# Loading each row of v once and copying the neighbour rows inside the v tile

## The chip, the cores and the metric

One core of one Trainium2 chip runs the whole program. The metric is the device time of one execution in microseconds. The kernel before took 333.7 us (median of 3 runs, 332.48 to 333.8).

## The reference, cut to what matters

Two stages follow each other. The first is attention in chunks: 4 batches, 8 heads, 768 positions, 64 numbers per head. A chunk of 32 queries sees its own 32 keys, 16 to the left, 8 to the right, and 8 memory keys of its head.

```python
for c in range(nc):                      # 24 chunks of 32
    l_start = max(0, c * 32 - 16)
    r_end = min(S, c * 32 + 32 + 8)
    k_full = concat([mem_k, k[:, :, l_start:r_end]])
    v_full = concat([mem_v, v[:, :, l_start:r_end]])
    a = softmax(scale * q_c @ k_full.T)
    out[:, :, c * 32:c * 32 + 32] = a @ v_full
```

The second stage is a mixture of 8 experts over the 3,072 tokens that come out (512 numbers each). Logits with noise choose two experts for each token, a softmax over the two gives their weights, and each expert is `relu(x @ w1) @ w2` with a hidden size of 1,024.

```python
noisy = x @ w_gate + log1p(exp(x @ w_noise)) * noise
top2 = the two largest per token; top2_w = softmax over the two
out[token] = sum over the two of top2_w * (relu(x @ w1[e]) @ w2[e])
```

## The kernel before

*Attention.* The 32 heads are taken in 8 groups of four heads, and a group in two pairs of heads. For a group, POOL issues the loads of q and k (L505, `qk_load`, 384 KB each as counted in the tile) and two loads of v (L516, `piece` inside `v_load`), one for each half of the partitions. All three convert from float32 to bfloat16 on the way.

The tile of v is `vg`, [128 partitions, 2, 48 chunks, 66]. A half has 64 partitions, and each partition is one position in the window of a chunk: 16 left neighbours, the chunk's 32 own positions, 8 right neighbours (`WIN` is 56 in all) and 8 memory rows. The third axis is the chunk: 24 of one head and 24 of the next. The last axis holds the 64 numbers of v, a column of ones (which gives the sum of the softmax) and a spare column. So the product with v for one chunk takes all its rows from one column block, and a position that is a neighbour of another chunk lies in the tile twice. The load writes all 56 rows of every chunk, so v's rows are read 56/32 times over. Where a window runs over the edge of the tensor, an extra short load takes its place (`first`, `last`).

Three v tiles (`NV = 3`) take turns, and so do three each of q and k. Group g + 3 uses the tile of group g, once the second pair's product has read it. At the start the tiles are cleared, and the column of ones is set.

The memory rows come from a copy that is already in SBUF (`memv`, inside the tile `XS`): two transfers of 49.5 KB for a group, issued by SyncE (SP) on its own DMA queue (L535, `mem_rows`).

For each pair, PE turns q and k (L555), makes the scores (L578 for memory, L585 for the window), DVE takes the maximum off (L592, L608), ACT takes the exponential (L611), PE turns the result (L617) and multiplies with v (L631, 24 products, one for a chunk), DVE normalises into `xrow` (L635, L647) and PE turns that for the logits (L656). After four pairs a batch is done and its routing follows (L693 to L907): logits, choice of two experts, places in a table. SP writes the batch's rows to `x_rows` in DRAM (L913).

*Experts.* When a table is ready, POOL gathers rows of `x_rows` (L949), PE turns them (L980) and multiplies with w1 (L1055), ACT or DVE takes the positive part (L1065, L1067), PE multiplies with w2 (L1096), DVE adds with the gate (L1107, L1115), and POOL scatters to the output (L1127). The weights w1 of the first two experts have tiles of their own (`w1t`, loaded on L927) beside the attention tiles; the other weight tiles (`w1l`, `w2l`) use memory that the attention leaves.

*The order.* A planner written in Python (`Planner.run`) lays all operations out ahead of time. Each has the engines that may do it with a duration, what it depends on (`deps`), what it must only be issued after (`after`), buffers that it takes and uses, and a priority. The priority is a formula plus a correction from the table `SHIFT` by name, and by name and running number. The instruction order of each engine, the DMA queues included, is the planner's, and the real waits are set by the data. `FETCH` is a part of the planner's model: per 128 products PE spends at least the third number of microseconds up to the time in the fourth, and the fifth number after it. A DMA has a transfer time and a latency in the model (`dma=`). The first w1 load is put after the list that group 5 keeps of its v operations, the second after that of group 7 (`groups[NG - 3][5]`, `groups[NG - 1][5]`). Before, that list is the two loads and the memory rows. The product with v depends on the same list.

Of the kernel before, what the change touches and what calls it, by code (L numbers as in the profile page):

```python
# [22 lines left out]
FETCH = (128, 94, 6.3, 97.0, 3.2)  # L23
SHIFT = {
# [183 lines left out]
def kernel(  # L208
# [14 lines left out]
    nc = tc.nc  # L223
    B, H, S, D = q.shape
    n_mem = mem_k.shape[2]
    chunk, left_ctx, right_ctx = 32, 16, 8
    ncnk = S // chunk
# [158 lines left out]
    z_v = []  # L386
# [111 lines left out]
    for g in range(NG):  # L498
# [11 lines left out]
        def v_load(o, hh, bv=bv, g=g, h0=h0, b=b):  # L510
            vt = bv.t
            hd = b * H + h0 + 2 * hh
            p0 = 64 * hh

            def piece(c, n, j=0, nj=WIN):
                G_.dma_start(out=vt[p0 + j:p0 + j + nj, hh, c:c + n, :D],  # L516
                             in_=bass.AP(v.tensor, v.offset + (hd * S + c * chunk + j - left_ctx) * D, [[D, nj], [chunk * D, n], [1, D]]))

            first, last = hd == 0, hd == B * H - 2
            if first:  # L520
                piece(0, 1, left_ctx, WIN - left_ctx)
            if last:
                piece(2 * ncnk - 1, 1, 0, WIN - right_ctx)
            piece(int(first), 2 * ncnk - first - last)
# [742 lines left out]
```

## Time and profile before

| What | us |
|---|---|
| profiled execution, its own time | 333.6 |
| its span, first to last instruction | 332.1 |
| PE busy (matmuls) | 282.3 |
| DVE busy | 159.8 |
| ACT busy | 147.9 |
| POOL busy | 131.3 |
| first product with v (L631) starts | 27.9 |
| first product of the experts (L1055) starts | 121.8 |

The table is read thus: times inside the execution count from the start of the span, and the execution's own time is 1.5 us longer than the span. Mean granted clock of PE over the span: 0.903. Of the DMA queues, the one that POOL issues to moved 38.78 MB in 74,672 packets, SP's queue 4.19 MB in 5,014.

### The profile page before, as it was taken

To read this page: it belongs to the slowest core of one execution; us is meant where nothing else is said; L and a number is where in the kernel's file an instruction comes from. 1 tells how busy PE (TensorE), PEld (TensorE's weight loads), DVE (VectorE), ACT (ScalarE), POOL (GpSimd) and SP (SyncE) were. 2 spreads that over 40 slices of the span, in tenths; PEclk is the share of its full clock that TensorE was granted. 3 is DMA by queue.
4 is the path that set the end of the run, shared out by engine and by line. 5 is a ranking of instruction groups with operands and counts; after the bars stand their busy time and mean duration, and the time that the engine had idled before them with its cause. 6 is when DMAs were issued, how large, how long until landed. Compare 5 with 4: busy or idle time off the path is not lost.

```text
span 332.1 us, 7279 instructions
## 1 busy us (share of the span) xinstructions
PE 282.3 (85%) x2972; PEld 177.1 (53%) x2972; DVE 159.8 (48%) x372; ACT 147.9 (45%) x261; POOL 131.3 (40%) x178
## 2 busy tenths in 40 slices
PE   0587588777567679999999999999999999999991
PEld 0575366665446456664646655545545744744540
DVE  7776677888748776824313431144042041043041
ACT  8675667888264134760611417403703604603500
POOL 7767533345000776987282410132032032051072
PEclk9999975978755558999999999999999999999998
DMA  7999999999999359289999910699613621021032
GB/s 100 208 128 139 149 150 149 212 171 195 223 183 116 89 127 177 79 140 188 247 210 227 248 68 0 106 182 198 101 54 78 99 79 57 2 109 51 3 122 82
DMA packets 80013, 43.55 MB, mean 131 GB/s; under 512 B 53805, under 2 KB 73262, under 8 KB 79974
## 3 DMA queue, kind: packets, MB, share of 16 engines
q0 software_dynamic: 74672, 38.78, 100.2%
q1 hardware_dynamic: 5014, 4.19, 4.9%
q8 instruction: 24, 0.39, 0.5%
q14 instruction: 15, 0.12, 0.1%
q10 hardware_dynamic: 288, 0.07, 0.1%
HBM read 61.26 MB, written 10.85 MB: 217 GB/s over the span
## 4 chain that ended last, share of the span: by engine, by line
PE 59%; DMA 21%; issue 8%; POOL 4%; DVE 4%; ACT 1%; POOLq 1%; DVEq 0%; ACTq 0%
PE ps_l L1055 20%; DMA vg<-in_v_dram 19%; PE ps_l L1096 18%; PE ps_g L1096 7%; PE ps_g L1055 7%; PE ps_l L980 2%; POOL out_dram L1127 2%; PE ps_o L631 2%; DMA kn<-in_k_dram 2%; PE ps_g L656 1%; DVE xrow L647 1%; POOL vg L516 1%; POOLq L1183 1%; PE ps_g L617 1%; PE ps_s L585 1%
## 5 line engine op out<-in xcount | busy, mean ns | idle before, releaser
L1065 ACT ACTIVATE ht<-ps_l 128x384 bf16<-128x384 f32 (+2 forms) x110 | 48.5, 491 | 95.0 <-PE ps_l L1055 94.0
L1096 PE MATMUL ps_l<-w2l,ht 128*128 128x512 bf16 x328 | 73.7, 379 | 0.0
L1096 PEld LDWEIGHTS <-ht 128*128 128x128 bf16 x448 | 43.6, 98 | 51.5
L1127 POOL DMA_INDIRECT out_dram<-acc,oid x28 | 28.8, 1028 | 84.9 <-DVE acc L1115 79.7
L1115 DVE SCALAR_TENSOR_TENSOR acc<-ps_l,gates,acc 128x512 f32<-128x512 f32 x22 | 16.5, 751 | 60.3 <-PE ps_l L1096 59.3
L1055 PEld LDWEIGHTS <-w1t 128*128 128x128 bf16 x416 | 31.4, 100 | 19.6 <-issue 2.2
L1055 PE MATMUL ps_l<-XS,w1t 128*128 128x384 bf16 (+4 forms) x312 | 40.7, 285 | 0.7 <-ACT XS L368 0.7
L1055 PEld LDWEIGHTS <-w1l 128*128 128x128 bf16 x320 | 29.9, 98 | 19.1
L1055 PE MATMUL ps_l<-XS,w1l 128*128 128x512 bf16 (+3 forms) x240 | 39.9, 316 | 0.0
L516 POOL DMA_DIRECT2D vg<-in_v_dram x18 | 23.7, 1317 | 23.3 <-DMA vg<-in_v_dram 10.7
L368 ACT COPY kT<-ps_q 64x768 bf16<-64x768 bf16 x31 | 24.6, 793 | 8.8 <-PE ps_q L555 8.2
L1096 PE MATMUL ps_g<-w2l,ht 128*128 128x512 bf16 x120 | 28.2, 379 | 0.0
L555 PE MATMUL ps_q<-identb,qn 128*64 128x128 bf16 x192 | 11.9, 276 | 15.6 <-POOL identb masks.py:199 10.6
L631 PE MATMUL ps_o<-vg,PT 128*32 128x132 bf16 x384 | 12.1, 279 | 9.0 <-DMA vg<-in_v_dram 5.0
L1107 DVE TENSOR_SCALAR acc<-ps_l,gates 128x512 f32<-128x512 f32 x13 | 9.8, 751 | 19.6 <-PE ps_l L1096 19.6
L1065 ACT ACTIVATE ht<-ps_g 128x384 bf16<-128x384 f32 (+2 forms) x38 | 16.8, 471 | 5.3 <-PE ps_g L1055 5.1
L949 POOL DMA_INDIRECT xl<-x_rows,gid x16 | 16.7, 1044 | 5.8 <-PE ps_l L980 2.2
L555 PEld LDWEIGHTS <-qn 128*64 128x64 bf16 x192 | 9.6, 147 | 16.6 <-DMA qn<-in_q_dram 12.6
L592 DVE TENSOR_REDUCE mx<-ps_s 128x12 f32<-128x768 f32 x16 | 15.3, 953 | 3.8 <-PE ps_s L585 3.4
L368 ACT COPY PT<-ps_g 128x768 bf16<-128x768 bf16 x13 | 10.3, 796 | 12.3 <-PE ps_g L617 11.2
L961 DVE COPY gates<-xl 64x8 f32<-64x8 f32 (+1 forms) x40 | 11.0, 292 | 9.9 <-DMA xl<-x_rows,gid 8.0
L647 DVE TENSOR_TENSOR xrow<-ps_o,rec 128x768 bf16<-128x768 f32 x16 | 15.3, 958 | 0.6
(179 smaller groups left out, 387.7 us busy)
## 6 DMA issues: line engine op xcount, KB each, us to landing
w2l<-in_moe_w_dram POOLq DMA_DIRECT2D x8, 1024.0 KB, 11.2
vg<-in_v_dram POOLq DMA_DIRECT2D x14, 336.0 KB, 20.9
w1t<-in_moe_w_dram POOLq DMA_DIRECT2D x4, 1024.0 KB, 22.3
w1l<-in_moe_w_dram POOLq DMA_DIRECT2D x4, 1024.0 KB, 10.5
kn<-in_k_dram POOLq DMA_DIRECT2D x8, 384.0 KB, 15.0
qn<-in_q_dram POOLq DMA_DIRECT2D x8, 384.0 KB, 18.7
x_rows<-xrow SPq DMA_DIRECT2D x2, 792.0 KB
x_rows<-xrow SPq DMA_DIRECT2D x2, 768.0 KB
```

The costliest lines, as they stand in the source:

```text
L368: A.copy(dst, src)
L516: G_.dma_start(out=vt[p0 + j:p0 + j + nj, hh, c:c + n, :D], in_=bass.AP(v.tensor, v.offset + (hd * S + c * chunk + j - left_ctx) * D, [[D, ...
L555: P_.transpose(out=dst.t[64 * hh:64 * hh + 64, t * QP:(t + 1) * QP], in_=s[:, j + 2 * hh, t, :], identity=identb)
L592: mx = op("mx", ("DVE", 0.98), lambda o, bmx=bmx, bS=bS: V.tensor_reduce(out=bmx.t, in_=sv(bS), axis=AX, op=Alu.max), deps=[sc], alloc=[bm ...
L631: P_.matmul(out=pvw[32 * r:32 * r + 32, u // UB, u % UB], lhsT=PT[:, u, 32 * r:32 * r + 32], rhs=vt[:, :, ncnk * j + c], start=True, stop= ...
L647: V.tensor_tensor(out=x5, in0=ov(bO)[:, :, :, :, :D], in1=r5.to_broadcast([128, 2, UB, 2, D]), op=Alu.mult)
L949: G_.indirect_dma_start(out=bx.t[:n], out_offset=None, in_=src, in_offset=bass.IndirectOffsetOnAxis(ap=ids_[:n, c:c + 1], axis=0), bounds_ ...
L1055: P_.matmul(out=dst, lhsT=w1b[e].t[:, kp, f * 128:(f + 1) * 128], rhs=src, start=(kp == 0), stop=(kp == KP - 1), skip_group_check=True)
L1065: A.activation(out=dst, in_=s_, func=Act.Relu)
L1096: P_.matmul(out=gy.t, lhsT=ht.t[:, f, j, :], rhs=w2b[e].t[:, f, :], start=(f == 0), stop=(f == FB - 1))
L1115: V.scalar_tensor_tensor(out=ba.t, in0=gy.t, scalar=gate, in1=ba.t, op0=Alu.mult, op1=Alu.add)
L1127: G_.indirect_dma_start(out=out_part[nv], out_offset=bass.IndirectOffsetOnAxis(ap=oid[:, c:c + 1], axis=0), in_=ba.t, in_offset=None, boun ...
```

## The change

Each v load now brings only the 32 own rows of a chunk, to the partitions 16 to 47 of its half, for all 48 chunks in one transfer; the extra short loads at the edges are gone. When a half has landed, SP issues two copies inside the tile. The first takes the last 16 of the own rows of chunk c (partitions 32 to 47) to the left neighbours (partitions 0 to 15) of chunk c + 1. The second takes the first 8 own rows (partitions 16 to 23) of chunk c + 1 to the right neighbours (partitions 48 to 55) of chunk c. Both move 47 chunks whole, 66 numbers each with the column of ones. The product with v now waits for the memory rows and the copies.

The planner's durations for the v load are changed, the copies are added to its list, `FETCH` has 6.9 in place of 6.3, and the table `SHIFT` is another one, so the order of nearly all instructions is new. The list of a group that the w1 loads are put after is now the memory rows and the two pairs of copies.

```diff
-FETCH = (128, 94, 6.3, 97.0, 3.2)
+FETCH = (128, 94, 6.9, 97.0, 3.2)
 SHIFT = {
...
         def v_load(o, hh, bv=bv, g=g, h0=h0, b=b):
             vt = bv.t
             hd = b * H + h0 + 2 * hh
-            p0 = 64 * hh
-
-            def piece(c, n, j=0, nj=WIN):
-                G_.dma_start(out=vt[p0 + j:p0 + j + nj, hh, c:c + n, :D],
-                             in_=bass.AP(v.tensor, v.offset + (hd * S + c * chunk + j - left_ctx) * D, [[D, nj], [chunk * D, n], [1, D]]))
-
-            first, last = hd == 0, hd == B * H - 2
-            if first:
-                piece(0, 1, left_ctx, WIN - left_ctx)
-            if last:
-                piece(2 * ncnk - 1, 1, 0, WIN - right_ctx)
-            piece(int(first), 2 * ncnk - first - last)
+            p0 = 64 * hh + left_ctx
+            G_.dma_start(out=vt[p0:p0 + chunk, hh, :, :D], in_=bass.AP(v.tensor, v.offset + hd * S * D, [[D, chunk], [chunk * D, 2 * ncnk], [1, D]]))
 
         zd = z_v[g] if g < NV else []
-        lv = [op("lv", ("POOL", 1.4 if 0 < g < NG - 1 else 2.2), lambda o, hh=hh, f=v_load: f(o, hh), deps=zd, alloc=[bv] if hh == 0 else [], use=[] if hh == 0 else [bv],
-                 prio=pr + 2 + 0.5 * hh, dma=(2.75, 1.6), tag="attn") for hh in range(2)]
+        lv = [op("lv", ("POOL", 1.05), lambda o, hh=hh, f=v_load: f(o, hh), deps=zd, alloc=[bv] if hh == 0 else [], use=[] if hh == 0 else [bv],
+                 prio=pr + 2 + 0.5 * hh, dma=(1.6, 1.6), tag="attn") for hh in range(2)]
...
-        groups.append((bq, bk, bv, lq, lk, lv + [lm]))
+
+        def spread(o, hh, bv=bv):
+            vt = bv.t[64 * hh:64 * hh + 64, hh]
+            nc.sync.dma_start(out=vt[:left_ctx, 1:], in_=vt[chunk:chunk + left_ctx, :2 * ncnk - 1])
+            nc.sync.dma_start(out=vt[left_ctx + chunk:WIN, :2 * ncnk - 1], in_=vt[left_ctx:left_ctx + right_ctx, 1:])
+
+        ln = [op("ln", ("SP", 0.3), lambda o, hh=hh, f=spread: f(o, hh), deps=[lv[hh]], after=[lm] if hh else [], use=[bv], prio=pr + 3 + 0.2 * (hh + 1), dma=(0.5, 1.8), tag="attn") for hh in range(2)]
+        groups.append((bq, bk, bv, lq, lk, [lm] + ln))
```

29 rows, old and new, of the table SHIFT are left out of this document.

## The prediction

> **What bounds the kernel now.** I read the page's slices first, then the busy times by stage, then the chain of waits, then the DMA queues. The slices, 8.3 us each:
>
> ```profile
> PE   0587588777567679999999999999999999999991
> DVE  7776677888748776824313431144042041043041
> PEclk9999975978755558999999999999999999999998
> DMA  7999999999999359289999910699613621021032
> ```
>
> From slice 15 on (about 122 us) PE is full: the experts. Before, nothing is full but the DMA engines, from 8 to about 98 us. So the change, which touches only the attention stage, is worth what it moves the start of the experts. The same by stage: length, then PE, PEld, DVE, ACT and POOL (busy us, instructions), clock, DMA share, GB/s:
>
> ```profile
> 27.86:81.64 53.78, 40.27 (x972) 32.94 (x972) 43.01 (x99) 39.17 (x56) 24.89 (x49) 0.82 2.45 167
> 59.29:81.64 22.35, 16.08 (x431) 13.46 (x422) 20.18 (x55) 19.09 (x28) 8.89 (x9) 0.88 1.91 197
> 81.64:98.68 17.04, 9.79 (x185) 8.08 (x182) 11.30 (x28) 7.62 (x13) 1.26 (x2) 0.60 1.91 205
> 98.68:121.78 23.10, 15.62 (x279) 12.66 (x279) 18.46 (x55) 7.97 (x14) 11.05 (x15) 0.50 0.77 114
> 121.78:127.50 5.72, 5.72 (x50) 4.03 (x50) 3.76 (x22) 1.58 (x4) 2.02 (x3) 0.50 0.90 107
> 127.50:325.00 197.50, 197.50 (x1255) 107.92 (x1253) 62.71 (x129) 71.04 (x160) 71.53 (x81) 1.00 0.57 118
> ```
>
> I cut the stages at PE's products with v (L631, 24 for a pair, 48 for a group): counted for that line alone, in the same stretches:
>
> ```profile
> 27.86:81.64 53.78, 7.31 (x240) 5.03 (x240) 0.82 2.45 167
> 81.64:98.68 17.04, 1.38 (x48) 0.93 (x48) 0.60 1.91 205
> 98.68:121.78 23.10, 3.41 (x96) 2.31 (x96) 0.50 0.77 114
> ```
>
> So groups 0 to 4 took 53.78/5 = 10.76 us each, group 5 took 17.04, and groups 6 and 7 with the end of the routing 23.10. The chain says what group 6 waited for:
>
> ```profile
> 48.42 20.39 DMA vg<-in_v_dram
> 71.15 27.49 DMA vg<-in_v_dram
> 98.68 0.85 PE ps_o L631 x18
> ```
>
> A v load issued at 71.15 lands 27.49 us later, and PE's product starts 0.04 us behind it. The groups before were slowed too, but less plainly.
>
> **The change, part by part.** *Loads.* A half load fell from 56 rows x 48 chunks = 2,688 pieces of 128 B to 32 x 48 = 1,536. What a piece costs, from two full stretches of 10 us (20 to 30, and 30 to 40):
>
> ```profile
> DMA packets 8222, 1.35 MB, mean 135 GB/s; under 512 B 7694, under 2 KB 8206, under 8 KB 8221
> q0 software_dynamic: 8189, 1.24, 303.6%
> q1 hardware_dynamic: 32, 0.10, 6.5%
> DMA packets 5537, 1.46 MB, mean 146 GB/s; under 512 B 4538, under 2 KB 5517, under 8 KB 5533
> ```
>
> With a for a small packet (v) and b for a middle one (q, k; 8206 - 7694 = 512 and 5517 - 4538 = 979): 7694a + 512b = 10 and 4538a + 979b = 10 give a = 0.90 ns, b = 6.1 ns. A half load thus costs 2.4 us of all engines, and 1.4 after: 1.03 saved, 2.06 for a group, 16.5 in all.
>
> [...]
>
> *Copies, added.* Per half one copy of 16 partitions and one of 8, whole rows of 47 x 66 x 2 = 6,204 B: 24 rows, 0.149 MB. Nearest row: the memory rows on the same queue, 0.10 MB in the 6.5% above (0.065 x 160 = 10.4 engine-us). By it a half's copies are 15.6 engine-us, 0.98 us of 16 engines if they ran alone, and 0.98/3.1 = 0.31 beside the 3.1 packets that are in flight per engine there. I take 0.5, nearer to the lower end since the loads do run beside it: 1.0 a group (0.6 to 2.0). Net per group -1.06 us of DMA time (-1.45 to -0.1).
>
> *Order of the w1 load.* It goes behind what the group's list ends with, which were load issues and is now the copies, planned behind the landing of the loads. Now, from POOL's timeline and the issues (KB, us to landing):
>
> ```profile
> 58.33 1.39 POOL L516 DMA_DIRECT2D vg<-in_v_dram  x1 [2.02 <-DMA vg<-in_v_dram]
> 60.48 0.78 POOL L927 DMA_DIRECT2D w1t<-in_moe_w_dram  x1
> 69.58 2.96 POOL L516 DMA_DIRECT2D vg<-in_v_dram  x2 [2.60 <-DMA vg<-in_v_dram]
> w1l<-in_moe_w_dram POOLq DMA_DIRECT2D x4, 1024.0 KB, 10.5
> ```
>
> The 1,024 KB go out at 60.48, right behind the loads of group 5 and ahead of the loads of group 6, which are late. The same size later, with the queue freer, lands in 10.5 us, so it is worth up to about 8 us of queue. Behind group 6's loads it costs nothing: the first expert product is at 121.78. With the 12 loads before group 6's second one (12 x 0.53 = 6.4) that is more than the 6.3 us by which group 5's stage is too long (17.04 - 10.76). I take the whole stall away: **-6.3** (0 to -6.3).
>
> *The pace of the other groups.* DMA time would let it fall by 1.06. DVE is busy 43.01/5 = 8.60 us per group, and where DMA pressed least (59.29 to 81.64) it was busy 20.18 of 22.35, 90%; at 90% a group takes 9.56, or 1.2 less than now. PE has a limit of its own:
>
> ```profile
> 33.34:41.40 8.06, 4.13 (x129) 3.13 (x129) 5.33 (x8) 5.00 (x7) 4.20 (x4) 1.00 2.78 150
> 41.40:48.69 7.29, 5.73 (x129) 4.90 (x129) 5.60 (x10) 4.96 (x8) 1.69 (x2) 0.77 2.86 149
> 41.40 0.35 PE L631 MATMUL ps_o<-vg,PT 128*32 128x132 bf16 x11 [2.29 <-issue]
> 48.69 0.30 PE L555 MATMUL ps_q<-identb,kn 128*64 128x128 bf16 x3 [1.20 <-issue]
> q8 instruction: 24, 0.39, 0.5%
> ```
>
> PE stops in the middle of a run of products, waiting for nothing that the profile shows, every 128 or so products, and a DMA queue named instruction brings 0.39 MB in 24 packets, 16 KB each. So PE's instructions come in blocks, and a block took 7.29 to 8.06 us while the engines were full. The copies do not lighten that, and the planner's figure for a block goes up from 6.3 to 6.9. Between no gain and 1.2 I take 0.7, nearer to what DMA and DVE allow, for each of seven groups: **-4.9** (0 to -8.4).
>
> *The first group.* It has no earlier work to hide the copies: SP waits for the second load, issues two copies (0.62 us each, as the memory rows on L535 below) and they land. The shortest landing that the trace has, of gathered rows, is 2.8 us. So +4.0, less the two shorter loads, 2.06: **+2** (-1 to +4). For later groups the copies lie under the groups ahead as long as v lands earlier than its use.
>
> ```profile
> L535 SPq DMA_DIRECT2D vg<-XS x16: 624/624/770, 11.5 to 74.9; - x16
> DMA to landing us min/median/max: 2.8/5.1/18.1
> 79.37 1.44 POOL L516 DMA_DIRECT2D vg<-in_v_dram  x1 [1.21 <-DMA vg<-in_v_dram]
> 86.50 34.95 SPq L913 DMA_DIRECT2D x_rows<-xrow  x4
> 109.75 1.17 POOL L949 DMA_INDIRECT xl<-x_rows,gid_s  x1 [14.22 <-DVE rec L635]
> ```
>
> *SP's queue.* SP now stands waiting for each half load, and behind it stand the next memory rows and the writes of x rows (L913). Their reader is the gather at 109.75. The last v load goes out at 79.37 and with the 20.9 us of the median (row under D) is in by about 100 even as things are, so the third write has some ten us of cover; I cost it at nothing, and without cover at what it is late. The 32 issues (20 us of SP) lie in SP's waiting. POOL's issues get shorter, but POOL is idle half of the time (24.89 of 53.78 busy): nothing.
>
> *The experts.* From 127.50 PE is busy all 197.50 us at full clock; their work is the same: nothing. The first 50 products run at clock 0.50 for 5.72 us, of which 2.9 could go if PE came warm; I take nothing.
>
> **Sum.** 333.6 us is the profiled execution's own time: a span of 332.1 and 1.5 around it, 0.1 under the median of the runs shown. 333.6 - 6.3 - 4.9 + 2.0 = **324.4**, say 324, with its own range 319 to 330.
>
> **The rivals.** *B, all of it gives.* The pace falls to DVE's 9.56 (-8.4), the stall goes (-6.3), the experts start warm (-2.9) and the first group one us sooner: 333.6 - 18.6 = 315. For it: a new order of everything, made for these costs; DMA share falls to 1.91 where loads are fewer and products come faster there (431 in 22.35 us, 6.6 us for 128). Against: DVE must stay at 90% throughout. [...]
>
> *C, PE's instructions bound.* From 27.86 to 121.78 PE does 972 + 185 + 279 = 1,436 products. At 8.06 us for 129 they take 89.7 us against 93.92 now: -4.2, +2 for the first group: 331.4. For it: the two stalls. Against: the pace of 59.29 to 81.64.
>
> *E, the copies eat it.* At 0.98 us a copy pair a group saves 0.1 us of DMA time; if the w1 load's place matters little, the stall stays: 333.6 + 2 - 0.7 = 334.9.
>
> *D, slower: the copies sit in the turn of the v tiles.* There are three; a tile is free only after its second pair's product. Group 3's first load goes out at 33.17 and group 6's, into the same tile, at 69.58. Loads now also need the copies to land, L us later, and two turns follow each other. Each costs L - 2.1 more. With L at half of a v load's 20.9 us, 10.5, as one of several queues under a full engine: 2 x 8.4 = +16.8, less the 9.2 of the forecast: 341. It decides from L = 2.1 + 9.2/2 = 6.7 us. Against: the shortest landing, 2.8.
>
> ```profile
> 33.17 1.41 POOL L516 DMA_DIRECT2D vg<-in_v_dram  x1
> vg<-in_v_dram POOLq DMA_DIRECT2D x14, 336.0 KB, 20.9
> ```
>
> **How the numbers follow.** Forecast 0.47, B 0.20, C 0.15, E 0.08, D 0.10. Something under 0.5% (1.7 us) is not told from no change here. Faster holds the forecast, B and two thirds of C: 0.78. Same holds E and the rest of C: 0.12. Slower is D: 0.10. The range leaves out D and the lower part of B: 313 to 334.
>
> **What would show it.** Right: no chain piece of a v load over 20 us, group 5's stage near 10 us, the first w1 load issued after group 6's v loads, the first L1055 product at 110 to 114 us, 197 us of full PE behind it. C: waits by "issue" through the whole stage, 7 to 8 us apart. E: slices of DMA at 9 to the same place. D: products at L631 waiting for vg written by SP, and v loads issued over 36 us after the loads three groups before. Wrong altogether, if the experts' start moves by ten us and the end does not.

## The result: the changed kernel is slightly slower, and its profile

The changed kernel took 337.2 us (median of 7 runs, 335.6 to 338.0) where the kernel before took 334.3 beside it: a ratio of 1.009, 95% interval 1.006 to 1.0119. A second measurement on another occasion gave 1.008 (0.9999 to 1.0162). A ratio takes the fast runs alone, those within 1.5% of the fastest of their kernel, so it need not be the quotient of the medians, and the profiles of three kernels (loads and copies in the old order, by pair of heads, four v tiles) are of slower runs. The forecast was 324, with a range of 313 to 334. The profiled execution took 337.19 us, its span is 335.7.

The slices of the changed kernel, 8.4 us each:

```profile
PE   0683575767475659999999999999999999999991
DVE  7683568897689886383243134043034023042141
PEclk9998769896795557999999999999999999999996
DMA  7999999999994249748999984884613612022022
```

PE fills up about where it did before, near slice 15, and what lies behind is the same. The DMA engines are full for slices 1 to 11, and then no longer. The page's queues and DMA issues (KB each, median us from issue to landing):

```profile
q0 software_dynamic: 50096, 36.40, 83.7%
q1 hardware_dynamic: 5782, 6.57, 9.4%
```

```profile
vg<-in_v_dram POOLq DMA_DIRECT2D x16, 192.0 KB, 16.3
...
vg<-vg SPq DMA_DIRECT2D x16, 96.9 KB
```

POOL's queue lost 24,576 packets and 2.38 MB; SP's queue gained 768 packets and the same 2.38 MB. A v load now lands in 16.3 us (20.9 before). So the transfers did become lighter, and the time still did not fall. The stages say where it went: length, then PE, PEld, DVE, ACT and POOL (busy us, instructions), clock, DMA share (packets under way on an engine at a time, on average, so it can be over 1) and GB/s; cut at the first product with v, at group 5's first product, at the first expert product, and 5.7 us later.

```profile
31.64:88.53 56.89, 37.18 (x903) 29.58 (x904) 41.74 (x86) 36.26 (x52) 15.00 (x18) 0.80 2.05 163
88.53:126.53 38.00, 25.00 (x495) 20.85 (x496) 31.77 (x98) 18.62 (x30) 12.40 (x16) 0.63 0.71 139
126.53:132.26 5.73, 5.73 (x51) 3.60 (x50) 5.09 (x31) 1.53 (x3) 1.51 (x2) 0.76 1.01 144
```

Before, these cuts lie at 27.86, 81.64 and 121.78. So the first product comes 3.8 us later, groups 0 to 4 take 3.1 us more (56.89 against 53.78), and the three last groups with the end of the routing take 2.1 us less (38.00 against 40.14): the experts start 4.8 us later. Behind that the span is 1.1 us shorter (209.2 against 210.3).

What PE waited for at its products with v, up to the experts (us in total, times, longest), and the chain of waits between 27 and 90 us (start, us, what):

```profile
PE ps_o L627 <- DMA vg<-vg: 15.7, 5, 4.8
```

```profile
27.02 20.94 DMA vg<-in_v_dram
47.98 0.54 SPq L530
48.57 8.86 DMA vg<-vg
57.57 0.85 PE ps_o L627 x24
...
63.37 17.39 DMA vg<-in_v_dram
80.77 0.54 SPq L530
81.36 7.04 DMA vg<-vg
88.53 0.85 PE ps_o L627 x24
```

`vg<-vg` are the new copies. A load lands, SP issues two copies (0.54 us for the first), and the last of them lands 8.86 and 7.04 us after the second issue; the product starts right behind it. Five products, in groups 0, 1, 2 and 5, wait 15.7 us for copies in all. The kernel before has no copies to wait for; its products waited 5.0 us for v loads.

### The profile page after: what moved, and what is told of

It reads as the page before. It is cut to its first block, busy times and chain, and to the rows that moved or that the text cites. A ratio compares the mean times of both kernels' runs of the same rounds, so it can differ in the third digit from the quotient of the medians.

```text
span 335.7 us, 7347 instructions
## 1 busy us (share of the span) xinstructions
PE 277.1 (83%) x2955; PEld 173.2 (52%) x2972; DVE 161.1 (48%) x370; ACT 146.0 (43%) x262; POOL 122.5 (36%) x177
## 4 chain that ended last, share of the span: by engine, by line
PE 55%; DMA 18%; DVE 9%; issue 8%; POOL 4%; ACT 2%; POOLq 2%; SPq 0%; DVEq 0%; ACTq 0%
PE ps_l L1092 19%; PE ps_l L1051 17%; DMA vg<-in_v_dram 11%; PE ps_g L1051 6%; PE ps_g L1092 5%; DMA vg<-vg 5%; POOL out_dram L1123 2%; PE ps_q L551 2%; DMA qn<-in_q_dram 2%; PE ps_o L627 1%; PE ps_l L976 1%; POOLq L1179 1%; DVE mx L588 1%; PE ps_g L652 1%; DVE xrow L643 1%
## 5 line engine op out<-in xcount | busy, mean ns | idle before, releaser
L1092 PE MATMUL ps_l<-w2l,ht 128*128 128x512 bf16 x341 | 78.2, 379 | 0.6
L1111 DVE SCALAR_TENSOR_TENSOR acc<-ps_l,gates,acc 128x512 f32<-128x512 f32 x26 | 19.5, 751 | 63.9 <-PE ps_l L1092 61.0
L1051 PEld LDWEIGHTS <-w1l 128*128 128x128 bf16 x320 | 29.8, 98 | 18.8
L1061 ACT ACTIVATE ht<-ps_g 128x384 bf16<-128x384 f32 (+2 forms) x41 | 18.7, 490 | 46.7 <-PE ps_g L1051 46.5
L1051 PE MATMUL ps_l<-XS,w1l 128*128 128x256 bf16 (+3 forms) x240 | 38.8, 314 | 0.0
L627 PE MATMUL ps_o<-vg,PT 128*32 128x132 bf16 x384 | 12.5, 284 | 18.0 <-DMA vg<-vg 15.7
L367 ACT COPY kT<-ps_q 64x768 bf16<-64x768 bf16 x28 | 22.2, 792 | 10.8 <-PE ps_q L551 10.5
L513 POOL DMA_DIRECT2D vg<-in_v_dram x16 | 15.3, 960 | 25.2 <-PE ps_o L627 22.4
L1092 PE MATMUL ps_g<-w2l,ht 128*128 128x512 bf16 x91 | 21.9, 379 | 0.3
L551 PE MATMUL ps_q<-identb,qn 128*64 128x128 bf16 x192 | 11.3, 273 | 10.5 <-DMA qn<-in_q_dram 9.9
L1103 DVE TENSOR_SCALAR acc<-ps_l,gates 128x512 f32<-128x512 f32 x14 | 10.5, 751 | 18.5 <-PE ps_l L1092 15.3
L627 PEld LDWEIGHTS <-PT 128*32 128x32 bf16 x384 | 8.5, 122 | 20.4 <-issue 18.8
L607 ACT ACTIVATE P<-sd 128x768 bf16<-128x768 f32 x16 | 13.5, 845 | 6.3 <-DVE sd L604 6.1
L604 DVE TENSOR_TENSOR sd<-ps_s,mx 128x768 f32<-128x768 f32 x16 | 15.3, 956 | 0.8
## 6 DMA issues: line engine op xcount, KB each, us to landing
w1t<-in_moe_w_dram POOLq DMA_DIRECT2D x4, 1024.0 KB, 20.9
vg<-in_v_dram POOLq DMA_DIRECT2D x16, 192.0 KB, 16.3
```

What stands on the lines that cost most here:

```text
L367: A.copy(dst, src)
L513: G_.dma_start(out=vt[p0:p0 + chunk, hh, :, :D], in_=bass.AP(v.tensor, v.offset + hd * S * D, [[D, chunk], [chunk * D, 2 * ncnk], [1, D]]))
L551: P_.transpose(out=dst.t[64 * hh:64 * hh + 64, t * QP:(t + 1) * QP], in_=s[:, j + 2 * hh, t, :], identity=identb)
L627: P_.matmul(out=pvw[32 * r:32 * r + 32, u // UB, u % UB], lhsT=PT[:, u, 32 * r:32 * r + 32], rhs=vt[:, :, ncnk * j + c], start=True, stop= ...
L1051: P_.matmul(out=dst, lhsT=w1b[e].t[:, kp, f * 128:(f + 1) * 128], rhs=src, start=(kp == 0), stop=(kp == KP - 1), skip_group_check=True)
L1061: A.activation(out=dst, in_=s_, func=Act.Relu)
```

## The experiments

The expectations speak of these theories. **O**: the new order is to blame, not the transfers. **W**: the copies cost what their bytes take of the DMA engines. **R**: the long rows of a copy are the trouble. **K**: the copies of 8 partitions are the dear ones. **T** (rival D of the prediction): what counts is how late the copied rows are there, and not their bytes. **C**: a copy of this shape is slow by itself. Four of the expectations call W theory B; the rivals B and C of the prediction are other things. Ratios are against the kernel before, which was run beside each kernel; its median was between 334.3 and 338.2 on the several occasions. The stage times below are from one profile for each kernel; two profiles of the changed kernel put the start of the experts at 126.53 and 127.59 us, so differences of one us say nothing there. Where a kernel has no copies, shorter ones, only one of the two, or copies to another tile, the neighbour rows that it doesn't write are left out of the result.

### Order, loads and copies, one at a time

*The copies taken out.*

```diff
-            nc.sync.dma_start(out=vt[:left_ctx, 1:], in_=vt[chunk:chunk + left_ctx, :2 * ncnk - 1])
-            nc.sync.dma_start(out=vt[left_ctx + chunk:WIN, :2 * ncnk - 1], in_=vt[left_ctx:left_ctx + right_ctx, 1:])
```

> The changed kernel with its whole order, but SP issues no copies: the neighbour rows of v are left out (they stay as cleared), so the products with v wait for the loads and the memory rows alone. Theory T (turn): the copies land 7 to 9 us after their issue, and this latency sits between load and product and in the turn of the three v tiles; the 15.7 us that PE waits for copies go, and the experts start at 112 to 118 instead of 126.5: 322 to 329. Theory B (bytes): the copies cost through the DMA time that they take; also 322 to 329, told apart by the run with short copies. Theory O (order): the new order puts the routing too late, the copies do little: 334 to 338.

327.25 us, ratio 0.9769 (0.9731 to 0.9807).

*The new order alone*: the 56-row loads of before (`piece`, `first`, `last`) in place of the 32-row ones, and no copies. This computes everything.

```diff
-            p0 = 64 * hh + left_ctx
-            G_.dma_start(out=vt[p0:p0 + chunk, hh, :, :D], ...)
+            p0 = 64 * hh
...
+            piece(int(first), 2 * ncnk - first - last)
...
-            nc.sync.dma_start(out=vt[:left_ctx, 1:], in_=vt[chunk:chunk + left_ctx, :2 * ncnk - 1])
...
```

> The changed kernel's order of all instructions, but with the v loads of before (56 rows) and no copies. It computes the same as before. Theory O: as slow as the changed kernel or slower, 336 to 342. Theory T: the copies' latency is gone but the loads are long again; 330 to 336, about the kernel before. Theory B: 330 to 336 as well.

333.41 us, ratio 0.9952 (0.993 to 0.9974): the order isn't to blame, and this is better than both kernels by a little. The stages of the two kernels, cut at the same events as above; first the new order alone:

```profile
28.03:84.24 56.21, 36.93 (x903) 29.61 (x904) 42.04 (x87) 36.95 (x53) 21.98 (x20) 0.79 2.57 161
84.24:121.82 37.58, 25.65 (x496) 21.38 (x496) 31.32 (x98) 18.76 (x30) 11.15 (x15) 0.60 1.09 161
```

and the changed kernel without copies:

```profile
26.71:78.83 52.12, 36.17 (x919) 29.26 (x908) 41.20 (x82) 37.11 (x54) 16.23 (x20) 0.84 1.93 160
78.83:116.68 37.85, 25.21 (x495) 21.07 (x495) 33.01 (x104) 19.99 (x32) 12.41 (x16) 0.61 0.55 121
```

So in the new order the experts start at 121.82 with 56-row loads (121.78 before the change), at 116.68 with 32-row loads, and at 126.53 with 32-row loads and copies: **the order gives nothing, the shorter loads give 5.1 us, the copies take 9.9.** By the ratios the same three are -1.6, -6.1 and +10.7 us (of 334.3). And the last stretch is 37.6 to 38.0 us in all three, whatever the loads are.

*Loads and copies in the old order.* The kernel before with the 32-row loads, and the four copies of a group issued behind its memory rows.

```diff
             for hh in range(2):
                 nc.sync.dma_start(out=bv.t[64 * hh + WIN:64 * hh + CTX, hh], in_=memv[64 * hh + n_mem * g:64 * hh + n_mem * (g + 1)])
+            for hh in range(2):
+                vt = bv.t[64 * hh:64 * hh + 64, hh]
+                nc.sync.dma_start(out=vt[:left_ctx, 1:], in_=vt[chunk:chunk + left_ctx, :2 * ncnk - 1])
+                nc.sync.dma_start(out=vt[left_ctx + chunk:WIN, :2 * ncnk - 1], in_=vt[left_ctx:left_ctx + right_ctx, 1:])
```

> The kernel before with its order, but with the loads of 32 rows and the copies, which SP issues right behind the memory rows of the same group. Theory O: the order was what cost, so this is faster than before: 324 to 331. Theory T: the copies' latency stands in this order too, with nothing planned for it: 335 to 343. Theory B: 330 to 337.

337.7 us, ratio 0.9955 (0.991 to 1.0001), with wide scatter (332.4 to 342.6). Loads and copies together are worth next to nothing in that order too; there also the chain has a landing of copies of 8.33 us.

*The 56-row loads and the copies*, in the new order: the changed kernel with the loads of before.

```diff
-            p0 = 64 * hh + left_ctx
+            p0 = 64 * hh
...
+            piece(int(first), 2 * ncnk - first - last)
```

> The changed kernel's order and its copies, but with the v loads of before (56 rows), so that the copies write again what is there. It computes the same. Against the run with old loads, this order and no copies (333.4) it measures the copies alone. Theory W: 2.39 MB more at about 150 GB/s are 16 us of DMA time, most of it on the path: 342 to 350. Theory T: the landings alone, 337 to 342.

358.74 us, ratio 1.0612 (1.0541 to 1.0683), 6.6% of the kernel before above the same loads without copies, some 22 us. By bytes, the copies' 2.38 MB at the 161 GB/s of this stage would be 15 us even if nothing hid them. Its chain of waits:

```profile
32.74 25.21 DMA vg<-in_v_dram
...
58.55 8.75 DMA vg<-vg
73.88 22.45 DMA vg<-in_v_dram
96.93 9.03 DMA vg<-vg
```

A copy lands nearly 9 us late again, behind loads that take 22 to 25 us: load and copies stand in series, and where the loads have no slack, all of it shows.

### Fewer bytes

*Copies of 6 chunks, and of 24 (`1:25` and `:24` in place of `1:7` and `:6`), in place of 47*; the other copy is cut likewise, here and in the diffs below.

```diff
-            nc.sync.dma_start(out=vt[:left_ctx, 1:], in_=vt[chunk:chunk + left_ctx, :2 * ncnk - 1])
+            nc.sync.dma_start(out=vt[:left_ctx, 1:7], in_=vt[chunk:chunk + left_ctx, :6])
...
```

> The changed kernel with copies of 6 chunks in place of 47 (792 B a row in place of 6,204 B), the same number of transfers at the same places; the other neighbour rows are left out. Theory T: the landing is a wait in the queue and not a matter of size, so nearly as before the cut: 335 to 338, PE's waits for copies still over 12 us. Theory B: nearly as without copies: 322 to 330.

> The changed kernel with copies of 24 chunks in place of 47, the same transfers at the same places; the other neighbour rows are left out. Theory W (bytes): the attention stage is bound by the bytes that the DMA engines move, and the copies' 2.39 MB cost as much as the loads that they replace; the time lies about half way between short copies (327.3) and the full change (about 337): 330 to 334. [...]

6 chunks: 327.29 us, ratio 0.977 (0.9731 to 0.9809). 24 chunks: 330.32 us, ratio 0.9748 (0.9692 to 0.9805). Half of the bytes cost nothing that can be measured, the whole costs some 3%: that is no straight line in the bytes. Nor is it the lateness by itself: T had put the kernel with 6 chunks at 335 to 338 us, with over 12 us of waits. Its products wait 3.9 us for copies, those of the kernel with 24 chunks 7.0, those of the changed kernel 15.7. Their first product with v does come late (28.96 and 30.07 us against 26.71 without copies), but groups 0 to 4 then take 49.7 and 50.4 us in place of 52.1, so it is caught up.

*One of the two copies alone.*

> The changed kernel with only the copies of the 16 left rows; the right neighbour rows are left out. Theory W: two thirds of the bytes, which the runs with a third and a half (0.975 each) and with all (1.009) put at 0.98 to 1.00. Theory K (the second copy of a half, on 8 partitions, is what makes the pair late): 0.97 to 0.98, as with the right rows alone.

> The changed kernel with only the copies of the 8 right rows; the left neighbour rows are left out. Theory W: a third of the copied bytes, so about a third of the way from no copies (327.3) to the full change (about 337): 329 to 332. [...]

Only the 16-row copies: 334.8 us, ratio 0.9988 (0.9935 to 1.004). Only the 8-row copies: 331.0, ratio 0.9751 (0.9665 to 0.9837). K falls: the 8-row copies alone are free. The 16-row copies have two thirds of the bytes and cost about 2%.

### More copies

*Each copy in two (at chunk 24), and in four, with the same bytes.*

```diff
+            for a, z in ((0, 12), (12, 24), (24, 36), (36, 2 * ncnk - 1)):
-            nc.sync.dma_start(out=vt[:left_ctx, 1:], in_=vt[chunk:chunk + left_ctx, :2 * ncnk - 1])
+                nc.sync.dma_start(out=vt[:left_ctx, 1 + a:1 + z], in_=vt[chunk:chunk + left_ctx, a:z])
...
```

> The changed kernel with each copy split in two by chunks (24 and 23): the same bytes, twice the transfers, rows of 3.1 KB. It computes the same. Theory W: the bytes are the same, so within 1% of the changed kernel, 334 to 340. Theory T: twice the transfers one behind the other on the same queue, so later landings and 341 to 350. Theory R (a row of 6.2 KB blocks an engine): smaller rows help, 329 to 333.

> The changed kernel with each copy split in four by chunks: the same bytes, four times the transfers, rows of 1.6 KB, 128 issues on SP. It computes the same. Theory R (a long row holds an engine while POOL's queue fills up behind it, so short rows land sooner): a ratio of 0.985 to 0.997 to the kernel before, PE's waits for copies under 6 us. Theory W (bytes alone): 1.00 to 1.015 as the changed kernel. Theory T (one landing after the other): 1.02 and more.

In two: 335.82 us, ratio 0.9956 (0.9927 to 0.9985). In four: 357.17, ratio 1.0626 (1.0523 to 1.073). R falls with the second: shorter rows, same bytes, 5% more than uncut, and the DMA engines have less to do (share 0.99 between 60 and 100 us, where the changed kernel has 1.73).

*The lateness without the bytes*: each copy in four, of 3 chunks each, a quarter of the bytes.

```diff
+            for a in (0, 12, 24, 36):
-            nc.sync.dma_start(out=vt[:left_ctx, 1:], in_=vt[chunk:chunk + left_ctx, :2 * ncnk - 1])
+                nc.sync.dma_start(out=vt[:left_ctx, 1 + a:4 + a], in_=vt[chunk:chunk + left_ctx, a:a + 3])
...
```

> The changed kernel with each copy issued as four copies of 3 chunks: as many issues by SP as with each copy cut in four, but a quarter of the bytes (the other neighbour rows are left out). Theory T (what counts is how late the rows are there): SP's eight issues per half put the last landing about 3.5 us later than two issues do, so it stays well above the kernel without copies: 335 us or more, 1.00 of the kernel before, products' waits for the copies 10 us or more. Theory W (what counts is the bytes): as with half or a sixth of the bytes, 327 to 331 us, ratio 0.975 to 0.985.

356.21 us, ratio 1.0691 (1.0632 to 1.0751): as slow as four pieces with all the bytes. SP's timeline for one half, and PE's waits:

```profile
20.47 0.56 SPq L531 DMA_DIRECT2D vg<-vg  x1
21.08 0.64 SPq L532 DMA_DIRECT2D vg<-vg  x1
...
24.44 0.54 SPq L531 DMA_DIRECT2D vg<-vg  x1
25.02 0.64 SPq L532 DMA_DIRECT2D vg<-vg  x1
```

```profile
PE ps_o L628 <- DMA vg<-vg: 25.6, 7, 7.2
```

The eighth issue of a half ends 5.2 us after the first began, where two take 1.2. Groups 0 to 4 take 71.1 us, with a DMA share of 1.07; SP is issuing for 26.8 of the 29.9 us from 33.0 to 62.9. What is lost here is time on SP's way to the landing, not DMA capacity. Against the kernel without copies, half the bytes in two long copies were free, and a quarter in eight short ones costs 9%.

*The bytes without the lateness*: the same copies at the same places, to free space in another tile (`xs`, an unused part of XS).

```diff
-            nc.sync.dma_start(out=vt[:left_ctx, 1:], in_=vt[chunk:chunk + left_ctx, :2 * ncnk - 1])
+            nc.sync.dma_start(out=xs[:left_ctx], in_=vt[chunk:chunk + left_ctx, :2 * ncnk - 1])
...
```

> The changed kernel with the copies' bytes in full, by the same queue at the same places, but written to free space in another SBUF tile, so that no product waits for them (the neighbour rows in the v tile are left out); the next load of a v tile still waits till its rows have been read. Theory T: the time of the kernel without copies, 326 to 329 us, ratio 0.975 to 0.985. Theory W: the time of the changed kernel, ratio 1.00 or more, and the products wait for v's loads instead.

332.27 us, ratio 0.9918 (0.9874 to 0.9961), between the two theories: 1.5% above the kernel without copies, 1.7% below the changed one. Its stages and the longest waits of PE:

```profile
26.72:82.25 55.53, 35.70 (x920) 28.57 (x907) 41.15 (x82) 37.31 (x54) 16.25 (x20) 0.85 2.05 165
82.25:119.83 37.58, 25.49 (x496) 21.16 (x495) 32.73 (x104) 19.98 (x32) 12.05 (x16) 0.62 0.90 160
```

```profile
PE ps_s L575 <- issue: 5.0, 1, 5.0
...
PE ps_o L628 <- issue: 4.0, 2, 2.9
PE ps_s L582 <- issue: 3.6, 1, 3.6
```

The first product is back where it is without copies (26.72 against 26.71), and groups 0 to 4 take 3.4 us more than without. So **of the 9.9 us that the copies cost, 3.2 come from their transfer alone** (119.83 - 116.68) **and 6.7 from waiting for it** (126.53 - 119.83); of the latter 4.9 us are there already at the first product (31.64 - 26.72). By the ratios the split is more even, 5.0 us for the transfer and 5.8 for the wait, so the split is only a rough one. What PE waits for in this kernel carries no name in the profile (`issue`).

The 4.9 us of the first product do not last. At the first products of groups 0 to 5 the changed kernel is 4.9, 6.2, 5.8, 0.8, 3.3 and 6.3 us behind this one. At group 3 (first line the changed kernel, second this one) the two are nearly level, since this one has had its stop of 5.0 us just before; the changed kernel loses again at groups 4 and 5. Their loads wait for the v tiles of groups 1 and 2 and go out 3.7 and 1.1 us later than here (47.71 against 44.00, 62.41 against 61.29), and group 5's product waits for copies on top. The last two lines show it in the changed kernel: group 2's second product, then group 5's loads.

```profile
64.34 0.53 PE L627 MATMUL ps_o<-vg,PT 128*32 128x132 bf16 x24
63.53 0.63 PE L628 MATMUL ps_o<-vg,PT 128*32 128x132 bf16 x24
61.27 0.53 PE L627 MATMUL ps_o<-vg,PT 128*32 128x132 bf16 x24
62.41 1.88 POOL L513 DMA_DIRECT2D vg<-in_v_dram  x2 [1.67 <-PE ps_g L733]
```

### The landing by itself

*Only pairs of copies*, each followed by a small DVE copy that waits for it; 47, 24 and 6 chunks in turn, first with nothing else under way, then with 12 v loads and 12 loads of q and k in POOL's queue.

> The kernel has only pairs of copies (47, 24 and 6 chunks, three times each), each pair waited for by a small DVE copy: first with nothing else on the DMA engines, then with 12 v loads of 32 rows and 12 q and k loads waiting in POOL's queue. Everything else of the computation is left out. Theory T (the copies of the changed kernel land late because they share the engines with POOL's transfers): with nothing else a pair of 47 chunks lands within about 3 us of its second issue, behind the loads it takes 6 to 9 us, and a pair of 6 chunks little over 1 to 2 us in both. Theory C (copies inside SBUF of this shape are slow by themselves): a pair of 47 chunks takes 6 us or more in both parts.

The chain of waits; the `vg<-vg` rows are the time from the start of the second issue to the landing, in the order 47, 24, 6:

```profile
5.37 2.80 DMA vg<-vg
...
9.06 2.18 DMA vg<-vg
...
12.12 1.79 DMA vg<-vg
...
39.38 7.65 DMA vg<-vg
...
47.91 5.74 DMA vg<-vg
...
54.53 5.42 DMA vg<-vg
...
60.78 6.85 DMA vg<-vg
...
68.67 5.97 DMA vg<-vg
...
75.52 5.66 DMA vg<-vg
```

The first three are those with idle engines; all nine such pairs of the run land after 1.8 to 2.9 us, and the six behind POOL's loads after 5.4 to 7.7. C falls. Eight times the bytes make 1.0 us of difference in the first case and 1.2 to 2.2 in the second, while the full queue adds 3.6 to 4.9 us to every size. The share of the engines' time was 0.17 in the first part and 2.14 in the second.

### The turn of the v tiles, and one half only

*Four v tiles in place of three*, with room made (two tiles each for q and k, four for turned x, five for gathered rows), and the control with that room and three tiles.

```diff
-    NGE, NQ, NV = 2, 2, 3
+    NGE, NQ, NV = 2, 2, 4
-    fill(pl.pool("q", 3), ...)
+    fill(pl.pool("q", 2), ...)
...
```

> The changed kernel with four v tiles in place of three; room is made with two q and two k tiles in place of three, four tiles for turned x in place of five, five for gathered rows in place of six, and the order planned anew with these. Theory T (the copies' landing counts because it stands in the turn of the three v tiles): products' waits for the copies fall to under 5 us, and the time is at least 5 us below that of the same kernel with three v tiles. Theory W (the copies cost what their bytes take of the engines, wherever they stand): within 2 us of it.

> The control for the kernel with four v tiles: the changed kernel with the same room made (two q and two k tiles, four for turned x, five for gathered rows) and three v tiles as before. Both theories: as the changed kernel or up to 6 us slower, since q and k have a tile less each; waits for the copies 12 us or more.

Four tiles 346.82 us, ratio 1.0361 (1.0278 to 1.0445); three 347.63, ratio 1.0438 (1.0339 to 1.0537). The two differ by 0.8 us where T asked for 5, and the intervals overlap. The waits for copies came out against both expectations, 11.8 us with four tiles and 4.0 with three. But making room alone cost some 3%, and the two orders were planned apart, so this decides nothing about the turn of the tiles.

*By pair of heads*: each load and copy cut into the two heads of a half, so that a pair waits only for its own; order planned anew.

```diff
-        lv = [op("lv", ("POOL", 1.05), ... for hh in range(2)]
+        lv = [op("lv", ("POOL", 0.8), ... for j in range(2) for hh in range(2)]
-            vt = bv.t[64 * hh:64 * hh + 64, hh]
+            vt = bv.t[64 * hh:64 * hh + 64, hh, ncnk * j:ncnk * (j + 1)]
...
```

> Loads and copies by pair of heads: four loads of 24 chunks for a group and eight copies of 23 chunks (rows of 3 KB), and the product of a pair waits only for its own; planned anew with a copy's issue at 1.2 us and its landing at 2.5. It computes the same. If the landing of the copies is what holds the groups up (T or R), a pair's copies start while the other pair's load runs: a ratio of 0.975 to 0.995. If bytes bind (W): 1.00 to 1.02.

341.4 us, ratio 1.0131 (1.007 to 1.0192): no better, and not the gain that T and R asked for. It issues twice as many loads and copies; products wait 7.1 us for loads and 3.6 for copies, and the experts start at 126.2.

*One half with copies, the other with its 56-row load.*

```diff
+            if hh == 0:
                 p0 = 64 * hh + left_ctx
...
+            else:
+                p0 = 64 * hh
...
+                piece(int(first), 2 * ncnk - first - last)
...
+            if hh == 0:
                 nc.sync.dma_start(out=vt[:left_ctx, 1:], in_=vt[chunk:chunk + left_ctx, :2 * ncnk - 1])
...
```

> The whole computation, in the changed order: the first half of each group loads 32 rows and is copied, the second half loads its 56 rows and has no copies. The copies of the first half (landing 1.2 us of issue and some 7 us after its load) then run beside the second half's load. Theory T (lateness): the second load takes up a good part of the copies' landing, so half of the 6.2 us that 32-row loads bring in this order is kept: 328 to 331.5 us for a kernel before of 334.4, ratio 0.980 to 0.991, waits for copies under 6 us. If the half's copies are as late for the products as two halves' copies: at or above the same order with 56-row loads, ratio 0.995 or more.

337.1 us, ratio 1.0067 (1.0037 to 1.0097). I expected the second half's load to cover a good part of the landing, and it didn't. Its chain, and PE's waits:

```profile
23.48 22.19 DMA vg<-in_v_dram
45.68 8.28 DMA vg<-vg
```

```profile
PE ps_o L642 <- DMA vg<-vg: 7.9, 4, 2.8
PE ps_o L642 <- DMA vg<-XS: 6.4, 1, 6.4
```

The half's copies still land 8.3 us after their load is in, for half of the gain. The wait of 6.4 us is put down to memory rows (`vg<-XS`), but it is the copies' too: it ends at 88.12, before group 5's first product, whose memory rows went out at 65.64 and whose copies went out at 79.54 and 80.13; the memory rows that land just then, issued at 85.94, are group 7's. So products wait some 14 us for half as many copies, nearly what they wait for all of them.

*The changed kernel again.*

> The changed kernel as it is, on the same chip as the next three, since the kernel before gave 334.3, 335.5 and 338.0 on three occasions. All theories: a ratio of about 1.009 to the kernel before.

338.75 us, ratio 1.008 (0.9999 to 1.0162); waits for the copies 14.4 us, landings in the chain 8.49 and 6.35.

## Why the prediction was wrong, step by step

The forecast put the start of the experts at 112.6 us (121.78 - 9.2); it is 126.53, 13.9 later, and the stage behind is 1.1 shorter, which makes the 12.8 us between 324.4 and 337.2. Three terms carry it, by the profiles of the kernels that differ in one part:

| Term | forecast | measured | by |
|---|---|---|---|
| order, with the stall of group 6 | -6.3 | 0.0 | order alone against before: 121.82 - 121.78 |
| shorter loads (pace -4.9, first group -2.1) | -7.0 | -5.1 | no copies against order alone: 116.68 - 121.82 |
| copies (first group) | +4.0 | +9.9 | changed against no copies: 126.53 - 116.68 |

The second and third lines can't be parted cleanly, since the pace of -4.9 was forecast with the copies' bytes taken off (1.0 us a group). With the 3.2 us of the copies' transfer put to the loads, the lines are -1.9 where -7.0 was forecast, and +6.7 for waiting where it was +4.0.

**"I take the whole stall away: -6.3" failed, and the event that it rests on came as forecast.** The first w1 load does go behind group 6's v loads (POOL's timeline):

```profile
68.01 1.81 POOL L513 DMA_DIRECT2D vg<-in_v_dram  x2 [3.72 <-PE ps_o L627]
69.81 0.78 POOL L923 DMA_DIRECT2D w1t<-in_moe_w_dram  x1
```

Group 5's stage is 8.2 us long (88.53 to 96.75) where it was 17.04. But I compared it with the other groups' 10.76 as if nothing else were done in the stall: PE did 185 products in it, only 48 of them with v, and DVE was busy for 11.30 us. What is taken out of the stall comes back behind it: with the routing, the last three groups take 38.0 us against 40.14, so the stall was worth 2.1. With the order alone they take 37.58, 2.6 less than before, and the groups ahead give it back (56.21 against 53.78). The engine with the least room in this stretch is DVE, busy 31.77 of 38.00 us (33.01 of 37.85 without copies); all its waits there of some length:

```profile
DVE rec L631 <- PE ps_o L627: 4.8, 4, 2.5
DVE tab L864 <- PE ps_g L861: 0.6, 1, 0.6
```

The row that could have warned me stood in the prediction: 11.30 + 18.46 = 29.8 us of DVE in the 40.1 us from 81.64 on. At the 90% that I allowed DVE elsewhere the stretch could have lost 7 us; it reached 84%. In the chain of waits this stretch is mostly the routing's DVE steps, dozens of 0.1 to 1 us one after the other.

**The copies' term was too small by 5.9 us.** It rested on two sentences. "The shortest landing that the trace has, of gathered rows, is 2.8 us": that is the landing with idle engines (2.80, 2.18 and 1.79 us in the kernel with copies alone), and the copies are issued while the engines are full. Behind full engines they land 5.4 to 7.7 us after the issue in that kernel, 7.0 to 8.9 in the chain of the changed one. The nearer row was in the trace of the kernel before: its memory rows, also inside SBUF and on SP's queue, which the step took for the copies' bytes but not for their landing. Up to 64 us they land 6.0 to 9.1 us after their issue, by the updates of their semaphores in the kept trace.

That the first group's +4.0 came near the measured 4.9 us is luck. The second load is in at 22.8 (SP issues its copies at 22.79), and the product starts at 31.64, 8.8 us later, more than twice the 4.0. But "it has no earlier work to hide the copies" was wrong too: without copies the product starts at 26.71, so PE's other work hid 3.9 of the 8.8. For the same reason the shorter loads gave back 1.3 us there and not 2.1.

And "for later groups the copies lie under the groups ahead as long as v lands earlier than its use": the condition doesn't hold. In the new order products wait 10.6 us for v loads of 56 rows, nothing for loads of 32 rows without copies, and 15.7 us for the copies behind them: the shorter loads bring a lead, and the copies' landing is longer than it. The kernel before already had such waits at three of its eight groups (5.0 us). I had one of them in hand (the chain piece of 27.49 us that ended in the product) and read it as the w1 load's doing alone.

**The bytes.** I took 0.5 us of DMA time a half, with bounds of 0.31 and 0.98, 16 halves: 8.0 us (5 to 15.7). Measured with nobody waiting, they cost 3.2 us at the start of the experts (5.0 by the ratios), at or under the lower bound; half of them cost nothing. This term wasn't the mistake.

**The shorter loads** by themselves gave 5.1 us for 7.0, though not through a pace at DVE's limit: groups 0 to 4 fell from 56.21 to 52.12 us, 0.8 a group (I had 0.7), and the first product came 1.3 us sooner (I had 2.1). The groups after them gained nothing (37.85 against 37.58 us); the DMA share there is 1.09 even with the long loads. The count of pieces was wrong: the step reckoned with 1,152 fewer for a half load, and POOL's queue lost 1,536 packets (24,576 in 16), as many as if the 56 rows had been 64.

**SP's queue** at nothing, **the experts** at nothing: about right; the experts' stage is 1.1 us shorter, its first 5.73 us at a clock of 0.76 in place of 0.50. But "the 32 issues lie in SP's waiting" holds only for 32: with 128 they set the time (356.21 and 357.17 us).

**The rivals.** D named the mechanism (the copies' landing in series with the load, deciding from 6.7 us), and its landing of 10.5 us was nearer to the measured 7.0 to 8.9 than my 2.8. It expected the loss in two turns of the three v tiles, with loads over 36 us after those three groups before. For groups 3 and 6, which it named, that isn't so: 36.47 and 68.01, 31.5 us. But group 5's loads go out at 62.41, 38.8 us after group 2's first at 23.57 (29.9 before the change, 35.0 without copies), and the chain shown with the result is that turn: group 2's load and its copies, 8.86 us, the product, group 5's load into the same tile and its copies, 7.04 us. So D was nearer than its 0.10 says: one turn of the tiles where it had two. E came nearest in time (334.9), by a wrong way: it left the stall in place and let the copies' bytes eat the loads' gain. B and C asked for a gain that didn't come; but C's wait is there, unnamed stops of PE up to 5.0 us, once copies are no longer waited for. The chances add to 0.77 for faster and 0.13 for same, where I wrote 0.78 and 0.12.

**What stays open.** Neither theory alone forecast the runs. T failed with 6 chunks, with each copy in two, by pair, with four tiles, with one half and with nobody waiting; W failed with each copy in four, short or whole, with nobody waiting and, by the ratio, with 24 chunks; the copies behind 56-row loads cost more than either said. Half of the copies' bytes, and the 8-row copies alone, cost nothing, though they land nearly as late (7.25 and 6.78 us in their chains). One reading fits these runs: a wait for copies first takes the place of an unnamed stop of PE. Unnamed stops from 26 us to the experts are 10.0 us without copies, 4.4 with 24 chunks and 1.7 in the changed kernel; with the waits for copies added (0, 7.0 and 15.7) that makes 10.0, 11.4 and 17.4. What the stops are is not shown, and no run tests this reading. And each copy cut in two, with twice the issues and the same bytes, was about 1.3% faster than uncut (0.9956 against 1.009, intervals apart); groups 0 to 4 took 53.64 us in place of 56.89. Neither lateness nor bytes explains that.

## What to carry to other kernels

The copies that were added behind a load were in series with it here, and landed 7.0 to 8.9 us after their second issue in the chain, where idle engines gave 1.8 to 2.9. So price an added transfer at its landing under the load that the engines have at that moment, not at its bytes and not at the shortest landing in the trace; look for a transfer of the same kind on the same queue in the same stage. Then ask how much lead its reader has. The stall on PE that I took away whole, 6.3 us, was worth 2.1, with DVE busy for 31.77 of the 38.00 us: look at what the engine next in line has free, and count the work that was done during the stall before its length goes into a sum. Taking apart order, loads and copies, one kernel each, told in three profiles what no single profile told.

## What the runs showed of the hardware

A pair of copies inside SBUF on SP's queue lands 1.8 to 2.9 us after its second issue with idle engines (DMA share 0.17), and 5.4 to 7.7 us after it behind POOL's loads (share 2.14); from 6 to 47 chunks of 132 B in each of 24 rows make only 1.0 to 2.2 us of that. I had not expected POOL's loads to add 3.6 to 3.9 us even to the smallest: it lands 1.79 us after its second issue with idle engines, and 5.42 and 5.66 us after it behind the loads. What it waits for there the runs don't show.

One issue of such a copy takes SP mostly 0.54 to 0.64 us. Eight of them for a half (5.2 us, the copies of 3 chunks in four) kept SP issuing for 26.8 of 29.9 us in the attention stage, and PE waited 25.6 us for copies there at a DMA share of 1.07.
